# A mixer block on one Trainium2 core: five of seven column pairs of the MLP's first product as blocks of seven products

## The chip, the cores and the metric

One of the eight cores of a Trainium2 chip runs the whole kernel. The time is the device time of one execution in microseconds. Five engines work side by side, each on its own queue of instructions in program order: TensorE (PE; its weight loads are PEld) multiplies, VectorE (DVE), ScalarE (ACT) and GpSimd (POOL) work on elements, and SyncE (SP) issues most of the transfers. GpSimd issues those that add to what lies at their destination. SBUF holds the operands in 128 partitions; TensorE writes to PSUM, in banks of 512 float32 columns.

## What is computed

```python
x = A_x                                              # (1, 2048, 512)
h = x + attention(layernorm(x), wqkv, w_phi, wo)     # linear attention, 32 heads of 16
n = layernorm(h)
u = gelu(einsum("bsd,sf->bdf", n, w1) + b1)          # w1 (2048, 1792): over the tokens
y = einsum("bdf,fs->bds", u, w2) + b2                # w2 (1792, 2048)
out = h + transpose(y)
```

The MLP mixes tokens: its first product contracts 2048 tokens into 1792 features for each of 512 channels, its second contracts the features back into tokens. All is float32. A product is made of three passes of TensorE: each operand is split into a rounded high part (ScalarE's copy) and the rest (a subtraction, on VectorE or GpSimd), and high x high, high x low and low x high are summed in PSUM.

## The kernel before

The tokens stand in 16 tiles of 128, the features in 14 column tiles of 128. The work goes in four stages.

*Projections.* Keys, values and queries, with the layer norm folded into the weights. These are the same in both kernels.

*Attention, passes `it` = 0 to 17* (the loop over `it`). A pass works on several token tiles at once: `s_tr` and `s_num` make the numerators of a tile, `s_ol` its low part, `s_wo` the output projection into a bank `po` (L66 to L68, `mm3`), `s_h` adds the residual into `h` (L634) and stores it, and one pass later `s_moments`, `s_rstd` and `s_hn` normalize the tile and split it into `hs` (L61 and L62), one 128 x 512 operand for each of the high and the low part. The numerators and the projection share one bank, so the next `pn` waits for `s_h`. In the same passes `fill` already runs the MLP's first product for the first two column pairs: six products of 512 columns a call. The order on PE, DVE, ACT and POOL is the written one here.

*First product.* For each of seven pairs of column tiles `fill` runs through all 16 token tiles, 3 x 2 products of 512 columns for each. The weights come in by `stream` on SP's queue, ScalarE rounds them (L663), VectorE takes the rest (L670). `gelu` (L797) reads the finished banks; `operands_u` makes of the four quarters of a pair's result seven operands of 256 columns, by four subtractions (on GpSimd for the first two pairs, L804 to L807, and on VectorE for the others), and splits them.

*Second product.* Pairs of 128 x 128 blocks in both directions are multiplied by Strassen's and Winograd's scheme, with seven products of 256 columns in place of eight. `STEPS` are 8 pairs of token tiles x 7 pairs of feature tiles. `w2_sums` loads the raw blocks of two steps and makes three further sums in four operations (L854 to L857), `w2_parts` splits them, seven blocks of two steps at a time (L875, 1792 columns). `pair_of_tiles` multiplies: two of the products go by `narrow` (L913, three passes of 256 columns), five by `wide` (L921 with the high and the low part side by side, 512 columns, and L924, 256). The last pair of token tiles is all `narrow`. After a pair's seventh step VectorE and ScalarE sum the six banks (L972 to L988), and GpSimd issues adding stores of the result to `out` (L991, L992). `last_h` loads the last two tiles of `h` before the loop. Behind the attention the order is made by a planner, with `in_order` pinning the later part.

Of the kernel before, what the change touches and what calls it, by code (L numbers as in the profile page):

```python
# [17 lines left out]
P = 128  # L18
# [13 lines left out]
LAG = 3  # L32
WARM = 10
# [4 lines left out]
def block_kernel(ctx: ExitStack, tc: tile.TileContext, x, xT, wT, phic, wo, w1, b1, w2, b2,  # L38
# [34 lines left out]
    wqp = aq.enter_context(tc.tile_pool(name="wqp", bufs=1, side="right"))  # L73
    wqh = wqp.tile([P, KD, D], F32R, name="wqh")
    wql = wqp.tile([P, KD, D], F32R, name="wql")
    kvB = wqp.tile([P, 2, P], F32, name="kvB")
    kvS = wqp.tile([P, 4, 64], F32, name="kvS")
    sums = wqp.tile([P, SUMS, NPR, 2, 2], F32, name="smq")
    wqp.tile([P, 504], F32, name="pad")
# [378 lines left out]
    ms.enter_context(tc.manual_schedule(engines={ET.PE, ET.DVE, ET.Activation, ET.Pool}))  # L458
# [112 lines left out]
    ps_f = ctx.enter_context(tc.tile_pool(name="ps_f", bufs=2, space=PSUM, reuse_waits="tile"))  # L571
    wst = ExitStack()
# [5 lines left out]
    HN, HT, PHT, OS, PO, VE = {}, {}, {}, {}, {}, {}  # L578
# [68 lines left out]
    def s_hn(t):  # L647
        hn = ak.tile([P, D], F32, name="hn")
# [23 lines left out]
    def stream(src, k0, n, c0, w):  # L672

        raw = wf.tile([P, n, w], F32, name="wraw")
        wh_ = wf.tile([P, n, w], F32R, name="whi")
        wl_ = wf.tile([P, n, w], F32R, name="wlo")
# [44 lines left out]

    for it in range(NT + 2):
# [21 lines left out]
        if 0 <= it - 2 < NT:  # L744
            s_rstd(it - 2)
        if it + 3 < NT:
            s_ez(it + 3)
# [9 lines left out]
        run(sm if ql else sm[1:])  # L757
        if it > 0 and it + 2 < NT:
            run(s_den(it + 2, ps_t, "tr"))
        if 0 <= it - 1 < NT:  # L760
            s_wo(it - 1)
        for w in work[1:]:
            w()
        if 0 <= it - 1 < NT:
            s_h(it - 1)
        flush(1)
    flush()
    ms.close()
    a2.close()
    aq.close()  # L770

    NP = NF // 2
    HD = D // 2
    up = ctx.enter_context(tc.tile_pool(name="up", bufs=1, side="right", reuse_waits="tile"))
    uo = ctx.enter_context(tc.tile_pool(name="uo", bufs=2, side="right", reuse_waits="tile"))
    ws = ctx.enter_context(tc.tile_pool(name="ws", bufs=2, side="right", reuse_waits="tile"))
    ur = ctx.enter_context(tc.tile_pool(name="ur", bufs=4, side="right", reuse_waits="tile"))
    ut = ctx.enter_context(tc.tile_pool(name="ut", bufs=1, side="right", reuse_waits="tile"))
    ps_b = ctx.enter_context(tc.tile_pool(name="ps_b", bufs=4, space=PSUM, reuse_waits="tile"))
    NEAR = 2
    near = [up.tile([P, 7, 2, HD], F32R, name=f"un{p}") for p in range(NEAR)]  # L790
    up.tile([P, 120], F32, name="pad")
    U, UB, far = {}, {}, {}
# [7 lines left out]
    def operands_u(p):  # L800
        u = U[p]
        tt = ut.tile([P, 3, HD], F32, name="tt")
        e = nc.gpsimd if p < NEAR else nc.vector
        e.tensor_sub(tt[:, 0], u[:, 0], u[:, 1])  # L804
        e.tensor_sub(u[:, 0], u[:, 2], u[:, 0])
        e.tensor_sub(tt[:, 1], u[:, 2], tt[:, 0])
        e.tensor_sub(tt[:, 2], u[:, 3], tt[:, 1])  # L807
        if p < NEAR:
            for n0, src in ((0, u), (4, tt)):
                o = near[p][:, n0:n0 + src.shape[1]]  # L810
                split(o[:, :, 0], o[:, :, 1], src, nc.vector)
            for m in range(7):
                UB[p, m] = near[p][:, m]
            return
        for m in range(7):
            at = (p - NEAR) * 7 + m
            if at % 2 == 0:
                far[at // 2] = big.tile([P, 2, 2, HD], F32R, name="uf", tag="big")
            UB[p, m] = far[at // 2][:, at % 2]
            split(UB[p, m][:, 0], UB[p, m][:, 1], u[:, m] if m < 4 else tt[:, m - 4], nc.vector)  # L820

    for p in range(NP):
        while FN[p] < NT:
            fill(p, ps_b)
        for c in range(2):
            gelu(2 * p + c, PU[p][c])
        if p < NEAR:
            operands_u(p)
    for p in range(NEAR, NP):
        operands_u(p)  # L830
    wst.close()
    hp = ctx.enter_context(tc.tile_pool(name="hp", bufs=1, reuse_waits="tile"))

    STEPS = [(sp, p) for sp in range(NT // 2) for p in range(NP)]
    GRP = 2
    AW, RAW = {}, {}
    QUEUE = {}

    def in_order(*ops):

        for op in ops:
            with ExitStack() as st:
                for ins in QUEUE.values():
                    st.enter_context(tc.issue_after(ins))
                ins = op().ins
            QUEUE[ins.engine] = ins

    def w2_sums(g):
        other = g > AHEAD + 2 and g % 4 == 1
        raw = RAW[g] = (hp if other else ws).tile([P, GRP, 7, P], F32, name="wraw", bufs=1 if other else 3)  # L850
        for i, (sp, p) in enumerate(STEPS[g * GRP:(g + 1) * GRP]):
            nc.sync.dma_start(raw[:, i, 0:4].rearrange("p (k i) s -> p k (i s)", k=2),
                              w2v[:, 2 * p:2 * p + 2, sp * 2 * P:(sp + 1) * 2 * P])
        sums = (lambda: nc.vector.tensor_add(raw[:, :, 4], raw[:, :, 0], raw[:, :, 2]),  # L854
                lambda: nc.vector.tensor_sub(raw[:, :, 5], raw[:, :, 4], raw[:, :, 1]),
                lambda: nc.vector.tensor_sub(raw[:, :, 0], raw[:, :, 1], raw[:, :, 0]),
                lambda: nc.vector.tensor_sub(raw[:, :, 6], raw[:, :, 3], raw[:, :, 5]))  # L857
        if g < AHEAD:
            with tc.issue_after(LO[-18]):
                for op in sums:  # L860
                    op()
        else:
            in_order(*sums)

    def w2_parts(g):
        home = hp if g % 3 == 2 else ws
        wh_ = home.tile([P, GRP, 7, P], F32R, name="whi")
        wl_ = home.tile([P, GRP, 7, P], F32R, name="wlo")
        for i, step in enumerate(STEPS[g * GRP:(g + 1) * GRP]):
            AW[step] = wh_[:, i], wl_[:, i]  # L870
        raw = RAW.pop(g)
        if g < AHEAD:
            split(wh_, wl_, raw, nc.vector)
        else:
            in_order(lambda: nc.scalar.activation(wh_, raw, AF.Copy), lambda: nc.vector.tensor_sub(wl_, raw, wh_))  # L875

    AHEAD = 2
    for g in range(AHEAD):
        w2_sums(g)
        w2_parts(g)  # L880
    for g in range(AHEAD, AHEAD + 2):
        w2_sums(g)
    parts_next, sums_next = [], []

    def stream_w2(n):

        if (n + 1) % NP == 0:
            for g in sums_next:
                w2_sums(g)
            sums_next.clear()  # L890
        if n % GRP == 0:
            parts_next.append(n // GRP + AHEAD)
        if (n + 2) % NP == 0:
            return
        for g in parts_next:
            if g * GRP < len(STEPS):
                w2_parts(g)
            if (g + 2) * GRP < len(STEPS):
                if (n + 3) % NP == 0:
                    sums_next.append(g + 2)  # L900
                else:
                    w2_sums(g + 2)
        parts_next.clear()


    P1, P2, P3, P4, P5, P6, P7 = (1, 1), (3, 3), (6, 2), (2, 6), (4, 4), (5, 5), (0, 0)

    def narrow(o, ps, m, sp, opens, closes):

        for p in ps:  # L910
            wh_, wl_ = AW[sp, p]
            for i, (x, y) in enumerate(((wh_, 0), (wh_, 1), (wl_, 0))):
                in_order(lambda: nc.tensor.matmul(o, x[:, m[0]], UB[p, m[1]][:, y], start=opens and p == 0 and i == 0,  # L913
                                                  stop=closes and p == NP - 1 and i == 2, skip_group_check=True))

    def wide(sp, p, *products):


        wh_, wl_ = AW[sp, p]
        for o, m in products:  # L920
            in_order(lambda: nc.tensor.matmul(o, wh_[:, m[0]], UB[p, m[1]], start=p == 0, stop=False,  # L921
# [11 lines left out]
    def pair_of_tiles(sp, p):  # L933
# [6 lines left out]
        if t + 2 == NT:  # L940
            if p < NP - 3 or end:
# [5 lines left out]
                if end:  # L947
                    last_sums(t, HB)
# [126 lines left out]
```

## Time and profile before

| | |
|---|---|
| time, median of 2 runs | 519.69 us (519.3 to 520.09) |
| span of the profiled execution | 517.9 us |
| its time beside the span | the median is 1.8 us above the span; the profile has no time of its own beside this |
| TensorE busy | 513.2 us |
| VectorE busy | 395.0 us |
| ScalarE busy | 285.3 us |
| GpSimd busy | 235.9 us |
| granted TensorE clock | 1.00 throughout |
| transfers | 57.66 MB |

The span is from the first instruction to the last. A busy time counts overlapping matmuls once; a matmul of 512 columns has a duration of 0.39 us because it is pipelined, and the next one starts well before it ends. So the price of a matmul is the distance between two starts. The second product begins at about 376 us, the attention ends at about 262 us.

### The profile page before, as it was taken

How to read it: one execution, taken by the hardware profiler on the slowest of the kernel's cores; microseconds unless marked ns; L12 is line 12 of the kernel's file. 1: busy time of each engine (PE TensorE's matmuls, PEld its weight loads, DVE VectorE, ACT ScalarE, POOL GpSimd, SP SyncE). 2: the span in 40 equal slices, each digit the busy share in tenths (PEclk: the TensorE clock that was granted, in tenths of full speed). 3: DMA queues.
4: the chain of work that ended last, by engine and by line, in shares of the span. 5: the costliest groups of instructions: out<-in, count | busy, mean ns of one | idle time of the engine just before them, and what ended most of it. 6: DMA issues, size and time to landing. Idle time of an engine off the chain costs nothing.

```text
span 517.9 us, 9772 instructions
## 1 busy us (share of the span) xinstructions
PE 513.2 (99%) x3761; PEld 434.0 (84%) x3761; DVE 395.0 (76%) x719; ACT 285.3 (55%) x501; POOL 235.9 (46%) x182
## 2 busy tenths in 40 slices
PE   9999999999999999999999999999999999999997
PEld 8888888888887777777788888888899999999997
DVE  6799889989987899697336624625797899888993
ACT  6999853526267877767756423425464434433530
POOL 3579997876999999974224000000001102110210
PEclk9999999999999999999999999999999999999999
DMA  8642301021302334333255433532134586557732
GB/s 311 209 142 84 102 22 42 1 83 44 122 27 97 103 103 119 107 103 123 82 163 162 123 94 90 184 102 62 41 115 94 141 201 136 139 156 181 137 48 61
DMA packets 46493, 57.66 MB, mean 111 GB/s; under 512 B 4080, under 2 KB 33136, under 8 KB 46448
## 3 DMA queue, kind: packets, MB, share of 16 engines
q1 hardware_dynamic: 43136, 51.38, 31.4%
q0 software_dynamic: 3024, 5.51, 7.6%
q8 instruction: 29, 0.48, 0.4%
q10 hardware_dynamic: 288, 0.17, 0.1%
q14 instruction: 16, 0.13, 0.1%
HBM read 46.81 MB, written 10.22 MB: 110 GB/s over the span
## 4 chain that ended last, share of the span: by engine, by line
PE 97%; DVE 1%; ACT 1%; issue 0%; DVEq 0%
PE pu L66 13%; PE pu L68 12%; PE pu L67 12%; PE py L921 11%; PE py L913 10%; PE py L924 6%; PE po L66 3%; PE pk_ps L66 3%; PE po L68 3%; PE po L67 3%; PE pk_ps L67 3%; PE pk_ps L68 3%; PE pv L67 3%; PE pv L66 3%; PE pv L68 3%; PE tr L591 2%
## 5 line engine op out<-in xcount | busy, mean ns | idle before, releaser
L991 POOL DMA_DIRECT2D out<-ot x14 | 12.5, 941 | 170.3 <-DVE ot L972 170.3
L66 PE MATMUL pu<-hs,whi 128*128 128x512 f32 x224 | 87.7, 394 | 0.0
L67 PE MATMUL pu<-hs,whi 128*128 128x512 f32 x224 | 87.2, 389 | 0.0
L68 PE MATMUL pu<-hs,wlo 128*128 128x512 f32 x224 | 86.5, 389 | 0.0
L670 DVE TENSOR_TENSOR wlo<-wraw,whi 128x512 fp32r<-128x512 f32 x56 | 46.9, 841 | 46.5 <-ACT whi L663 46.2
L875 ACT ACTIVATE whi<-wraw 128x1792 fp32r<-128x1792 f32 x26 | 44.0, 1704 | 30.9 <-issue 17.4
L663 ACT ACTIVATE whi<-wraw 128x512 fp32r<-128x512 f32 x56 | 34.6, 625 | 44.4 <-PE pu L67 39.4
L875 DVE TENSOR_TENSOR wlo<-wraw,whi 128x1792 fp32r<-128x1792 f32 x26 | 52.4, 2019 | 0.0
L66 PEld LDWEIGHTS pu<-hs,whi 128*128 128x128 f32 x224 | 42.0, 188 | 9.1 <-ACT hj L641 0.2
L68 PEld LDWEIGHTS pu<-hs,wlo 128*128 128x128 f32 x224 | 42.0, 188 | 8.9
L67 PEld LDWEIGHTS pu<-hs,whi 128*128 128x128 f32 x224 | 42.1, 188 | 8.5
L921 PE MATMUL py<-uf,whi 128*128 128x512 f32 x175 | 48.4, 395 | 0.0
L484 POOL TENSOR_TENSOR ez<-eq,zB 128x1024 f32<-128x1024 f32 x16 | 38.4, 2405 | 3.8 <-ACT zB L544 3.8
L913 PE MATMUL py<-uf,whi 128*128 128x256 f32 x210 | 39.0, 283 | 0.0
L213 POOL TENSOR_TENSOR pk<-pk,sk 128x1024 f32<-128x1024 f32 x16 | 31.1, 1949 | 11.2 <-DVE sk L212 10.0
L508 POOL TENSOR_TENSOR eq<-eq,w 128x1024 f32<-128x1024 f32 x16 | 32.4, 2026 | 3.2 <-DVE w L505 3.2
L921 PEld LDWEIGHTS py<-uf,whi 128*128 128x128 f32 x175 | 30.1, 189 | 3.9
L913 PEld LDWEIGHTS py<-uf,whi 128*128 128x128 f32 x210 | 32.8, 192 | 0.0
L217 POOL TENSOR_TENSOR zacc<-zacc,pk 128x1024 f32<-128x1024 f32 x13 | 31.4, 2412 | 0.5
L924 PEld LDWEIGHTS py<-uf,wlo 128*128 128x128 f32 x175 | 27.1, 189 | 3.8
L913 PE MATMUL py<-uf,wlo 128*128 128x256 f32 x105 | 29.7, 283 | 0.0
L924 PE MATMUL py<-uf,wlo 128*128 128x256 f32 x175 | 28.7, 281 | 0.0
(200 smaller groups left out, 1303.9 us busy)
## 6 DMA issues: line engine op xcount, KB each, us to landing
wraw<-in_w SPq DMA_DIRECT2D x112, 256.0 KB, 3.0
xraw<-in_xT SPq DMA_DIRECT2D x16, 256.0 KB, 2.9
xh<-in_x SPq DMA_DIRECT2D x16, 256.0 KB, 2.6
h<-in_x SPq DMA_DIRECT2D x16, 256.0 KB, 2.7
out<-h SPq DMA_DIRECT2D x16, 256.0 KB, 2.1
out<-ot POOLq DMA_DIRECT2D x14, 256.0 KB, 4.4
wraw<-in_wT SPq DMA_DIRECT2D x12, 256.0 KB, 5.1
out<-low POOLq DMA_DIRECT2D x7, 256.0 KB, 4.2
```

The lines of the kernel that those rows point to most:

```text
L66: nc.tensor.matmul(o, ah, bh, start=first, stop=False)
L67: nc.tensor.matmul(o, ah, bl, start=False, stop=False)
L68: return nc.tensor.matmul(o, al, bh, start=False, stop=last).ins
L217: nc.gpsimd.tensor_add(zacc, zacc, PK[t])
L484: nc.gpsimd.tensor_mul(EZ[t], EQ[t], zB)
L508: nc.gpsimd.tensor_mul(heads(EQ[t]), heads(EQ[t]), W[t].rearrange("p g c h -> p (g c h)").unsqueeze(2).to_broadcast([P, 2 * H, DH]))
L663: nc.scalar.activation(wh_, raw, AF.Copy)
L670: LO.append(nc.vector.tensor_sub(wl_, raw, wh_).ins)
L875: in_order(lambda: nc.scalar.activation(wh_, raw, AF.Copy), lambda: nc.vector.tensor_sub(wl_, raw, wh_))
L913: in_order(lambda: nc.tensor.matmul(o, x[:, m[0]], UB[p, m[1]][:, y], start=opens and p == 0 and i == 0, stop=closes and p == NP - 1 and i ...
L921: in_order(lambda: nc.tensor.matmul(o, wh_[:, m[0]], UB[p, m[1]], start=p == 0, stop=False, skip_group_check=True))
L924: in_order(lambda: nc.tensor.matmul(o[:, 0], wl_[:, m[0]], UB[p, m[1]][:, 0], start=False, stop=p == NP - 1, skip_group_check=True))
```

## The change

The scheme of seven products now also takes five of the seven column pairs of the first product. Only the first two pairs (`PLAIN = 2`) still go by `fill`, up to token tile 14 in the attention's passes and with tile 15 after step 0. The other five run as 40 new steps in front of the 56 of the second product: 8 pairs of token tiles for each, 21 products of 256 columns per step (`products`), into four banks, of which there are two sets (`four_banks`). The first two row pairs of the second product go by `products` as well, interleaved; row pairs 2 to 6 go by `wide_step` as before, and the last by `last_step`.

For this the normalized tokens are kept unsplit too (`HF`), and their seven operands are made: `h_ops` (four subtractions of 256 columns for each pair of tiles, six on VectorE as a list `DQ` and two on GpSimd, four of the seven operands being the tile's own quarters, one of them replaced), and `h_parts`, which splits 768 columns of sums on ScalarE and VectorE and 256 columns on ScalarE and GpSimd (VectorE for pair 3).

The weight sums are fewer. `load_raw` loads a step's four blocks and one of them a second time (four transfers on SP's queue for two steps), `add_raw` adds two blocks to two of these on arrival (adding loads from GpSimd, two for two steps), and `w_sums` makes the remaining two sums on VectorE. `w_parts` splits one step at a time, two steps ahead, into three homes.

The gelu's operands come by `u_sums` (four subtractions on GpSimd for every pair) at fixed steps and `u_parts`. Everything behind the attention is in one written order on all five queues; a table `PENDING` says after which step what stands. The table of the gelu is loaded in pass 10.

```diff
+UR = 6
+PLAIN = 2
-        split(HN[t][:, 0], HN[t][:, 1], hn, nc.gpsimd)
+        split(HN[t][:, 0], HN[t][:, 1], hn, nc.gpsimd if t < NT - 1 else nc.vector)
...
+    def block_ops(e, v, t0, t1, t2):
+        return [lambda: e.tensor_sub(t0, v[0], v[1]), lambda: e.tensor_sub(v[0], v[2], v[0]),
+                lambda: e.tensor_sub(t1, v[2], t0), lambda: e.tensor_sub(t2, v[3], t1)]
+    STEPS = ([("u", p, j) for p in range(PLAIN, NP) for j in range(NT // 2)]
+             + [("y", sp, p) for sp, ps in ((0, (0, 1)), (1, (0, 1, 2, 3)), (0, (2, 3)), (1, (4, 5, 6)), (0, (4, 5, 6)))
+                for p in ps]
+             + [("y", sp, p) for sp in range(2, NT // 2) for p in range(NP)])
...
+        for k in range(2):
+            src, r, c = blocks(2 * g + k)
+            nc.sync.dma_start(RAW[g][:, k, 1:5].rearrange("p (k i) s -> p k (i s)", k=2),
+                              src[:, r:r + 2, c:c + 2 * P])
+            nc.sync.dma_start(RAW[g][:, k, 0], src[:, r + 1, c:c + P])
...
+            nc.gpsimd.dma_start(RAW[g][:, k, 0:2].rearrange("p i s -> p (i s)"), src[:, r, c:c + 2 * P],
+                                accum_op=ALU.add)
...
+        nc.vector.tensor_add(raw[:, :, 5], raw[:, :, 0], raw[:, :, 2])
+        nc.vector.tensor_add(raw[:, :, 6], raw[:, :, 4], raw[:, :, 5])
...
+        pool = (ws, ws2)[n % 3] if n % 3 < 2 else hp
+        PARTS[n] = pool.tile([P, 2, 7, P], F32R, name="wp")
+        split(PARTS[n][:, 0], PARTS[n][:, 1], RAW[n // 2][:, n % 2], nc.vector)
+    U_SUMS = {0: 25, 1: 29, 2: 35, 3: 37, 4: 39, 5: 41, 6: 44}
+    U_PARTS = {0: 33, 1: 35, 2: 37, 3: 39, 4: 41, 5: 43, 6: 46}
+    def h_parts(j):
+        v = HF.pop(j).rearrange("p i (k d) -> p (i k) d", k=2)
+        split(CB[j][:, :, 0], CB[j][:, :, 1], v[:, 1:4], nc.vector)
+        split(HN[2 * j][:, 0, 0:HD], HN[2 * j][:, 1, 0:HD], v[:, 0], nc.vector if j == 3 else nc.gpsimd)
...
     for it in range(NT + 2):
...
+        some(GQ, {14: 2, 15: 5, 16: 2}.get(it, 0))
...
+        if it in (11, 12):
+            load_raw(it - 11)
+        if it == 10:
+            nc.scalar.activation(mhalf[:, 1:2], mhalf[:, 2:3], AF.Gelu_apprx_tanh)
...
+        if it == 13:
+            for j in range(5):
+                DQ.extend(h_ops(j, nc.vector))
+            GQ.extend([lambda: add_raw(0)] + h_ops(5, nc.gpsimd) + [lambda: add_raw(1)])
+        if it == 15:
+            DQ.extend(h_ops(6, nc.vector))
+        if it == NT:
...
+            w_sums(0)
+            h_parts(0)
+            w_parts(0)
...
+    def products(n, banks, x, first, last):
+        a, b, c, d = banks
+        for o, m, opens in ((a[:, 0], P1, True), (a[:, 1], P6, False), (d[:, 0], P7, True), (b[:, 0], P5, True),
+                            (b[:, 1], P4, False), (c[:, 0], P3, True), (c[:, 1], P2, False)):
+            narrow(o, n, m, x(m[1]), first and opens, last)
...
+    at(len(STEPS) - 14, lambda: HB.extend(last_h(NT - 2)))
+    w_sums(1)
+    w_parts(1)
+    step(0)
+    for p in range(PLAIN):
+        fill(p)
+    load_raw(2)
+    load_raw(3)
+    h_parts(1)
+    add_raw(2)
+    some(h_ops(7, nc.gpsimd))
+    step(1)
+    for n in range(0, len(STEPS)):
+        if n > 1:
+            step(n)
+        w_parts(n + 2)
+        if n % 2 == 0:
+            load_raw(n // 2 + 4)
+            add_raw(n // 2 + 3)
+        else:
+            w_sums((n + 3) // 2)
+        if ready:
+            store()
+        for f in PENDING.pop(n, []):
+            f()
```

More of the change, by code (lines that the diff above doesn't have):

```diff
@@ L822, in block_kernel @@
[L822 to L861, printed above, removed]
-        else:
-            in_order(*sums)
@@ L865, in w2_parts @@
[L865 to L903, printed above, removed]
@@ L906, in block_kernel, with u_sums @@
[L906 to L919, printed above, removed]
+    def u_sums(p):
+        u, tt = U[p], hp.tile([P, 3, HD], F32, name="tt", bufs=2)
+        UT[p] = tt
+        some(block_ops(nc.gpsimd, [u[:, k] for k in range(4)], tt[:, 0], tt[:, 1], tt[:, 2]))
@@ new lines, in u_parts @@
+    def u_parts(p, i):
+        if i == 2:
+            o = cb_tile(p)
+            src = UT[p]
+        else:
+            o = big.tile([P, 2, 2, HD], F32R, name="uf", tag="big")
+            src = U[p][:, 2 * i:2 * i + 2]
+        for m in range(o.shape[1]):
+            UB[p, 2 * i + m] = o[:, m]
+        split(o[:, :, 0], o[:, :, 1], src, nc.vector)
+    for p in range(PLAIN):
+        while FN[p] < NT - 1:
+            fill(p)
+    a2.close()
+    cbb = ctx.enter_context(tc.tile_pool(name="cbb", bufs=1, side="right", reuse_waits="tile"))
@@ new lines, in block_kernel, with narrow @@
+    ps_b = ctx.enter_context(tc.tile_pool(name="ps_b", bufs=4, space=PSUM, reuse_waits="tile"))
+    for j in range(NT // 2):
+        if j not in CB:
+            CB[j] = cb_tile(j)
+    P1, P2, P3, P4, P5, P6, P7 = (2, 1), (4, 3), (6, 2), (3, 6), (0, 4), (5, 5), (1, 0)
+    def narrow(o, n, m, x, opens, closes):
+        wh_, wl_ = PARTS[n][:, 0], PARTS[n][:, 1]
+        for i, (w, y) in enumerate(((wh_, 0), (wh_, 1), (wl_, 0))):
+            nc.tensor.matmul(o, w[:, m[0]], x[:, y], start=opens and i == 0, stop=closes and i == 2, skip_group_check=True)
@@ new lines, in u_gelu, with y_out @@
+    def u_gelu(p):
+        for i in range(2):
+            v = flat(U[p][:, 2 * i:2 * i + 2])
+            nc.scalar.activation(v, v, AF.Gelu_apprx_tanh, bias=b1s[:, 2 * p + i:2 * p + i + 1])
+    def y_out(t, banks):
+        e, u3 = firsts(banks)
+        ot = ur.tile([P, 4, HD], F32, name="u")
+        for i, a in enumerate((u3, e)):
+            nc.vector.scalar_tensor_tensor(ot[:, 2 * i:2 * i + 2], banks[1 + i], b2s[:, t + i:t + i + 1], a,
+                                           op0=ALU.add, op1=ALU.add)
+        return [(t + i, ot[:, 2 * i:2 * i + 2]) for i in range(2)]
@@ L990, in pair_of_tiles @@
-        for i in range(2):
-            nc.gpsimd.dma_start(out[(t + i) * P:(t + i + 1) * P, :], flat(ot[:, i]), accum_op=ALU.add)
-        nc.gpsimd.dma_start(out[(t + 1) * P:(t + 2) * P, :], flat(low), accum_op=ALU.add)
+        if NP - 3 <= p < NP - 1:
+            return []
+        places = [(b16[:, 0], P1, True), (b16[:, 1], P6, False), (b7[:, 0], P7, True), (b5[:, 0], P5, True),
+                  (b4[:, 0], P4, True), (b3[:, 0], P3, True), (b2[:, 0], P2, True)]
+        for o, m, opens in places if end else places[5:] + places[:5]:
+            for k in range(2 if end else 0, -1, -1):
+                narrow(o, n - k, m, UB[p - k, m[1]], opens and p == 0, end and k == 0)
@@ new lines, in block_kernel, with later, at @@
+    PENDING = {}
+    def later(d, f):
+        PENDING.setdefault(now[0] + d, []).append(f)
+    now = [-3]
+    def at(n, f, *args):
+        PENDING.setdefault(n, []).append(lambda: f(*args))
+    for j in range(2, NT // 2):
+        at(j - 2, h_parts, j)
+    for p in range(PLAIN):
+        for c in range(2):
+            at(c + 3, gelu, 2 * p + c, PU[p][c])
+    for p, n in U_SUMS.items():
+        at(n, u_sums, p)
+    for p, n in U_PARTS.items():
+        at(n, u_parts, p, 0)
+        at(n, u_parts, p, 1)
+        at(n + 1, u_parts, p, 2)
@@ new lines, in block_kernel @@
+    at(len(STEPS) - 14, lambda: HB.extend(last_h(NT - 2)))
+    HB = []
+    w_sums(1)
+    w_parts(1)
+    step(0)
+    for p in range(PLAIN):
+        fill(p)
+    wst.close()
+    hp = ctx.enter_context(tc.tile_pool(name="hp", bufs=1, reuse_waits="tile"))
+    load_raw(2)
[5 more added lines that the diff above has]
+    for n in range(0, len(STEPS)):
+        now[0] = n
+        ready = len(STORES)
+        if n > 1:
[4 more added lines that the diff above has]
+            add_raw(n // 2 + 3)
+        else:
+            w_sums((n + 3) // 2)
[3 more added lines that the diff above has]
+            f()
```

288 lines of the change are left out of this document (171 added, 117 removed).

## The prediction

> **What bounds the kernel now.** I read the page first, then the chain of waits, then TensorE's timeline, then the other engines where the change lands.
>
> ```profile
> span 517.9 us, 9772 instructions
> PE 513.2 (99%) x3761; PEld 434.0 (84%) x3761; DVE 395.0 (76%) x719; ACT 285.3 (55%) x501; POOL 235.9 (46%) x182
> PE 97%; DVE 1%; ACT 1%; issue 0%; DVEq 0%
> ```
>
> TensorE is the bound from start to end, and there are almost no holes to fill: any gain must come from fewer or cheaper matmuls, and any wait of TensorE for operands is added to the time in full. So I price the matmuls first, by their spacing and not by their pipelined duration. The timeline gives eighteen products of 512 columns in a row, the chain the steps of the second product.
>
> ```profile
> 250.73 0.40 PE L66 MATMUL po<-woh,oh 128*128 128x512 f32 x1
> ...
> 254.60 0.39 PE L68 MATMUL pu<-hs,wlo 128*128 128x512 f32 x1
> ...
> 259.72 0.39 PE L68 MATMUL po<-woh,ol 128*128 128x512 f32 x1
> 378.17 1.15 PE py L921 x5
> 380.63 1.16 PE py L921 x5
> 496.79 17.65 PE py L913 x147
> ```
>
> 3.87 us over 17 gaps is 0.228 us for 512 columns; 17.65 / 147 is 0.120 us for 256 columns. A step of the second product is 2.46 us, an all-narrow step of 21 products 21 x 0.120 = 2.52 us.
>
> **Parts 1 and 2: the matmuls.** The first product loses ten of its fourteen column tiles: 10 x 16 x 3 = 480 products of 512 columns, 480 x 0.228 = 109.4 us. It gains five pairs x 8 steps x 21 = 840 narrow ones, 100.8 us. The first two row pairs of the second product turn narrow, 14 steps x 0.06 = 0.8 us more. TensorE's own work falls by 109.4 - 100.8 - 0.8 = 7.8 us. That is all that the arithmetic saves, because each narrow product carries 0.12 us for half the columns of 0.228.
>
> **What the operands cost.** The new steps want splits and sums that the plain fill did not. The groups by line and shape give their durations.
>
> ```profile
> L875 DVE TENSOR_TENSOR wlo<-wraw,whi 128x1792 fp32r<-128x1792 f32 x26 | 52.4, 2019 | 0.0
> L855 DVE TENSOR_TENSOR wraw<-wraw 128x256 f32<-128x256 f32 x28 | 11.9, 424 | 0.8
> L875 ACT ACTIVATE whi<-wraw 128x1792 fp32r<-128x1792 f32 x26 | 44.0, 1704 | 30.9 <-issue 17.4 <-PE py L913 8.7 <-DVE wraw L857 4.8
> L663 ACT ACTIVATE whi<-wraw 128x512 fp32r<-128x512 f32 x56 | 34.6, 625 | 44.4 <-PE pu L67 39.4 <-DVE wraw L856 2.1 <-issue 1.8
> L991 POOL DMA_DIRECT2D out<-ot x14 | 12.5, 941 | 170.3 <-DVE ot L972 170.3
> ```
>
> On VectorE 256 elements take 0.42 us and 1792 take 2.02, so 1.04 ns an element: 896 (`w_parts`, one per step) 1.09 us, 768 (`h_parts`, the third part of `u_parts`) 0.95, 512 0.69. On ScalarE 896 takes 0.95, 768 0.84. `w_sums` is two adds of 256, 0.85 us every second step. A GpSimd issue of an adding load holds GpSimd 0.9 us, and there is one per step.
>
> VectorE and GpSimd do not run freely beside each other. The two timelines show it:
>
> ```profile
> 254.34 0.69 DVE L670 TENSOR_TENSOR wlo<-wraw,whi 128x512 fp32r<-128x512 f32 x1
> 231.69 1.95 POOL L508 TENSOR_TENSOR eq<-eq,w 128x1024 f32<-128x1024 f32 x1 [0.43 <-DVE w L505]
> 232.17 2.01 DVE L670 TENSOR_TENSOR wlo<-wraw,whi 128x512 fp32r<-128x512 f32 x1
> 274.83 0.74 POOL L807 TENSOR_TENSOR tt<-u,tt 128x256 f32<-128x256 f32 x1
> 280.11 0.69 DVE L670 TENSOR_TENSOR wlo<-wraw,whi 128x512 fp32r<-128x512 f32 x1
> 280.27 1.12 POOL L804 TENSOR_TENSOR tt<-u 128x256 f32<-128x256 f32 x1 [4.70 <-DVE un L62]
> ```
>
> The same subtraction takes 0.69 us alone and 2.01 us when GpSimd's multiplication began before it: it ends just 0.54 us after that one. GpSimd's subtraction of 256 takes 0.74 alone and 1.12 behind VectorE's. Each waits out the other, so I add their times. [...]
>
> **Part 3: the end of the attention.** `h_ops` puts 28 subtractions (28 x 0.42 = 11.8 us) on VectorE and four (3.0 us) with four adding loads (3.6 us) on GpSimd into the last four passes, and the activation table of the gelu moves to pass 10.
>
> ```profile
> 242.57 0.68 DVE L618 TENSOR_TENSOR ol<-pn,oh 128x512 fp32r<-128x512 f32 x1
> 246.74 0.69 DVE L634 SCALAR_TENSOR_TENSOR h<-po,h 128x512 f32<-128x512 f32 x1 [3.50 <-PE po L68]
> 264.86 0.63 ACT L61 ACTIVATE hs<-hn 128x512 fp32r<-128x512 f32 x1
> 270.09 1.28 ACT L797 ACT_TABLE_LOAD   x1
> ```
>
> VectorE idles 3.5 us between `ol` and `h` of a pass, so the work fits by volume. But TensorE waits for `h` (it frees the bank for `pn`) and for `ol`, and a subtraction in front of either costs up to 0.42 us, or 1.3 with GpSimd's split under way: eight such waits at about half a microsecond, 4 us, and the table load 1 of its 1.28. SP's queue takes eight loads of raw weights in passes 11 and 12, between a store of `h` and a load of `x` that is wanted passes later; I put nothing for it. I take 5; bounds 0 (all slip into the idle time) and 9.
>
> **Part 4: the first eight block steps.** From 259.72 + 0.23 eighteen more fill products run to 264.0, where step 0 stands. Steps 0 to 7 and the last two fills (12 x 0.228) want 8 x 2.52 + 2.7 = 22.9 us of TensorE. The last token tile's normalized rows come at 265.5 (the ScalarE row at 264.86); three copies of block 0 now stand ahead of it on ScalarE (0.84 + 0.41 + 0.95), so it comes near 267.3. Behind it, in VectorE's written order: its own split 0.7, four `w_sums` 3.4, seven `w_parts` 7.6, seven `h_parts` 6.7 and one of 0.42; on GpSimd six splits of a block's first 256 columns (the quarter split) 4.4 and `h_ops(7)` 3.0. Together 26.2 us, so step 7's operands stand at 293.5, while TensorE would want them at 264.0 + 17.7 + 2.7 = 284.4. The loss is 9.1 us. The first to be seen should be step 2, whose quarter split stands on GpSimd behind two adding loads, `h_ops(7)` and two more adding loads, 3.6 + 3.0 us. Taken 9, bounds 4 (times do not add) and 12.
>
> **Part 5: the gelu's operands, steps 33 to 47.** Fifteen steps are 37.8 us of TensorE. VectorE has fifteen `w_parts` 16.4, eight `w_sums` 6.8, seven `u_parts` of 0.69 + 0.69 + 0.95 = 16.3 and `u_out` 2.7; GpSimd has five `u_sums` of four subtractions, 20 x 0.74 = 14.8. The sum is 57.0, 19.2 over. Weights are split two steps ahead, which hides 5.0 us: 14 us are lost. If GpSimd's part were free, 42.2 us against 37.8 would vanish in the 5.0: bounds 0 and 19.
>
> **Part 6: the wide steps.** VectorE's sums at the end of a pair are one burst:
>
> ```profile
> 426.31 0.42 DVE L981 TENSOR_TENSOR u<-py,e 128x256 f32<-128x256 f32 x1 [0.99 <-ACT e L979]
> ...
> 429.61 0.87 DVE L972 SCALAR_TENSOR_TENSOR ot<-py,b2s,e 128x256 f32<-128x256 f32 x2
> 411.02:497.00 85.98, 85.98 (x560) 78.41 (x560) 78.37 (x136) 36.48 (x38) 13.07 (x15) 1.00 0.63 144
> ```
>
> The burst is 4.2 us. Now the parts of step n+2 stand behind it (before, two groups were ready): 1.3 us until the first bank is done + 4.2 + 1.09 = 6.6 us after the step's start, wanted after 2 x 2.46 + 1.16 (five wide products first) = 6.1. That is 0.5 to 1 us for each of five pairs, 4. The first wide pair waits for banks that `y_out` frees, a copy and three sums late: 2. The last pair opens narrow and has no 1.16 in front: 2. `last_h`, now at step 82, makes VectorE wait in line for two loads of 256 KB (2.8 us by the next fence) that stand on SP's queue behind four others, in the middle of a burst: 4, bounds 1 and 6. Together 12, bounds 5 and 16.
>
> **Part 7: the transfers.** Rows of the issues, and of the queues between 411.02 and 497:
>
> ```profile
> q0 software_dynamic: 2160, 3.93, 32.4%
> q1 hardware_dynamic: 8704, 8.39, 30.4%
> u<-out SPq DMA_DIRECT2D x2, 256.0 KB, 2.8
> ```
>
> Plain loads cost 0.304 x 86 / 8.39 = 3.1 us of all sixteen engines per MB, adding stores 0.324 x 86 / 3.93 = 7.1. A wide pair of 17.3 us now loads 2.29 MB (7.1 us), stores 0.79 MB (5.6) and adds 0.92 MB, which no row prices: 2.9 us as plain loads, 6.5 as adding stores. That is 15.6 to 19.2 us of 17.3. The adds are nearer to the adding stores, but four raw groups in flight absorb the first excess: 3, bounds 0 and 13 (five pairs of 1.9, and the queue's lateness).
>
> **The sum.** 517.9 - 7.8 + 5 + 9 + 14 + 12 + 3 = 553.1 us of span. The median of the runs shown, 519.69, is 1.8 above the span, for what lies around it: 555 us.
>
> **The rivals.** *GpSimd's subtractions find gaps of their own.* VectorE waits about 0.95 us for ScalarE's copy before each split; if GpSimd fits there, part 5 falls to 1, part 4 to 5 and part 3 to 3, and the rest stays: 519.7 - 7.8 + 3 + 5 + 1 + 12 + 3 = 536 us. Against it: in parts 4 and 5 the queues are full. *The adding loads bound the wide steps*, 13 in place of 3: 565 us. For it the 7.1 us per MB, against it that VectorE's lateness already thins the demand. *TensorE stays the bound*: two steps of lead, the banks in two sets and the late gelu cover it all, so that of 43 us of waits under 10 remain; it is decided at step 2 and in steps 33 to 47, where everything must arrive within 2.52 us a step. Then 519.7 - 7.8 = 512 us, up to 522 with what remains. For it: GpSimd is idle in most of this stage and TensorE waited for nothing before. *The narrow products do not keep 0.120 us* with the new operands: at 0.135 the saving becomes 5 us of loss, and 568 with the waits; the 147 of the row above, same shapes, speak against it.
>
> **How the numbers follow.** The forecast, 540 to 563, gets 0.55; gaps on GpSimd 0.16; adding loads 0.10; TensorE bound 0.16; slower products 0.03. Two per cent, about what a measurement of this kernel can tell, is 509.3 to 530.1. The third rival reaches both sides: 0.05 faster, 0.11 within, and 0.03 of the second group also ends within. So 0.05, 0.14, 0.81. The range holds 8 of 10: low 524, high 570.
>
> **What would show it.** Right: TensorE's busy share falls to about 92%, with waits at step 2 for GpSimd's quarter split, a row of waits for VectorE's weight split in steps 38 to 47, and one for it near step 85; GpSimd's 256-element subtractions above 0.74 us. Wrong: a chain that is again 97% TensorE, weight splits ready two steps ahead through steps 33 to 47, or DMA engines over 95% busy with VectorE waiting for `RAW`.

## The result and the profile after

| | before | after |
|---|---|---|
| time, median of the runs shown | 519.69 us | 557.38 us (557.29 to 557.47) |
| ratio, 95% interval | | 1.0725, 1.0704 to 1.0745 |
| span of the profiled execution | 517.9 us | 555.4 us |

The changed kernel is 7% slower. The page, its lines for the span, the busy times and the granted clock:

```profile
span 555.4 us, 11271 instructions
PE 523.0 (94%) x4191; PEld 458.4 (83%) x4191; DVE 453.8 (82%) x742; ACT 307.4 (55%) x527; POOL 354.3 (64%) x310
PEclk9999999999999999998989999999799999999799
```

TensorE's busy share fell from 99 to 94%. The last line is new: before, the granted clock was full throughout; now four slices show an 8 or a 7. A matmul at half clock still counts as busy (from 258.90 to 265.73 us TensorE is busy for 6.00 of the 6.83 us at a clock of 0.50), so the busy time overstates the work. The waits, TensorE's (waiting line, releaser, total us, times, longest us):

```profile
PE py L920 <- DVE wp L66: 7.3, 6, 2.6
PE py L929 <- DVE wp L66: 6.2, 5, 4.9
PE py L920 <- POOL hs L66: 5.0, 1, 5.0
PE pn L615 <- DVE h L640: 4.4, 3, 2.8
```

These are the four places that the prediction names. Of the first row 5.3 us lie in steps 40, 42 and 46, where VectorE's weight split stands among the gelu's operands; of the second 4.9 us lie in step 85, behind `last_h`; the third is GpSimd's quarter split at step 2, and the fourth the residual add in the attention. Before, TensorE had no wait like the first three, and this of the fourth kind:

```profile
PE pn L609 <- DVE h L634: 0.2, 1, 0.2
```

Where the time lies is read from the stretches. The first line below is the attention's last product into `po` in TensorE's timeline, which started at 259.72 before. Each line under it is a stretch: its bounds and its length, the busy us of PE, PEld, DVE, ACT and POOL, the clock, and the DMA share and GB/s. The bounds are starts of steps: 0, 8, 33, 48, the first wide pair, and the last pair.

```profile
267.08 0.39 PE L72 MATMUL po<-woh,ol 128*128 128x512 f32 x1
271.40:304.20 32.80, 26.84 (x181) 25.12 (x180) 26.13 (x28) 20.26 (x34) 20.65 (x21) 0.90 0.64 144
304.20:367.20 63.00, 63.00 (x527) 63.00 (x526) 46.01 (x69) 28.10 (x34) 30.15 (x34) 1.00 0.82 184
367.20:415.30 48.10, 41.48 (x318) 40.71 (x317) 46.61 (x55) 27.39 (x40) 32.76 (x34) 0.93 0.63 144
415.30:430.40 15.10, 15.10 (x127) 15.10 (x127) 12.33 (x20) 6.72 (x9) 7.06 (x8) 1.00 0.72 160
430.40:531.20 100.80, 92.03 (x563) 80.69 (x562) 71.21 (x122) 37.80 (x54) 43.84 (x50) 0.97 0.99 209
531.20:555.40 24.20, 18.70 (x149) 17.79 (x147) 14.84 (x28) 6.42 (x9) 2.98 (x4) 1.00 0.38 64
```

Steps 8 to 32 and 48 to 53 run with no gap: 25 steps in 63.0 us, 2.52 us each. The rest is longer than TensorE's own work:

| stretch | own work or before, us | after | excess | of it half clock |
|---|---|---|---|---|
| to the last `po` | 259.7 | 267.1 | 7.4 | 3.0 |
| steps 0 to 7, with the last fills | 22.9 | 32.8 | 9.9 | 2.8 |
| steps 33 to 47 | 37.8 | 48.1 | 10.3 | 3.0 |
| five wide pairs | 86.0 | 100.8 | 14.8 | 2.6 |
| last pair and the end | 20.9 | 24.2 | 3.3 | 0 |

The excess is 45.7 us; less the 7.8 us of work saved that is 37.9, and the spans differ by 37.5. The last column counts the time that TensorE worked at half clock, halved (products of 512 columns start 0.43 us apart there, in place of 0.228): the record of the clock shows 0.5 for 6.83 us from 258.9, 286.2, 395.4 and 518.3 us on, and the waits under way there ended at 259.7, 287.4, 396.3 and 520.1. This column is a reckoning, and not what a full clock would have gained: in steps 33 to 47 VectorE is busy for 46.6 of the 48.1 us, so a faster TensorE would have waited longer there.

### The profile page after: what moved, and what is told of

It reads as the page before. It is cut to its first block, busy times and chain, and to the rows that moved or that the text cites. A ratio compares the mean times of both kernels' runs of the same rounds, so it can differ in the third digit from the quotient of the medians.

```text
span 555.4 us, 11271 instructions
## 1 busy us (share of the span) xinstructions
PE 523.0 (94%) x4191; PEld 458.4 (83%) x4191; DVE 453.8 (82%) x742; ACT 307.4 (55%) x527; POOL 354.3 (64%) x310
## 5 line engine op out<-in xcount | busy, mean ns | idle before, releaser
L65 ACT ACTIVATE wp<-wraw 128x896 fp32r<-128x896 f32 x96 | 89.5, 949 | 136.1 <-PE py L920 50.8
L775 POOL DMA_DIRECT2D wraw<-in_w x96 | 87.9, 1050 | 91.3 <-DMA wraw<-in_w 50.4
L66 DVE TENSOR_TENSOR wp<-wraw,wp 128x896 fp32r<-128x896 f32 x96 | 106.5, 1126 | 44.7 <-ACT wp L65 44.7
L920 PE MATMUL py<-cb,wp 128*128 128x256 f32 x654 | 106.5, 289 | 0.6 <-DVE cb L66 0.6
L920 PEld LDWEIGHTS py<-cb,wp 128*128 128x128 f32 x654 | 92.4, 198 | 1.0 <-DVE cb L66 1.0
L920 PE MATMUL py<-hs,wp 128*128 128x256 f32 x480 | 72.9, 287 | 5.0 <-POOL hs L66 5.0
L920 PEld LDWEIGHTS py<-hs,wp 128*128 128x128 f32 x480 | 65.2, 196 | 5.6 <-POOL hs L66 5.2
L920 PE MATMUL py<-uf,wp 128*128 128x256 f32 x357 | 59.1, 292 | 8.9 <-DVE wp L66 7.3
L920 PEld LDWEIGHTS py<-uf,wp 128*128 128x128 f32 x357 | 50.6, 199 | 10.5 <-DVE wp L66 8.6
L218 POOL TENSOR_TENSOR pk<-pk,sk 128x1024 f32<-128x1024 f32 x16 | 31.0, 1943 | 11.2 <-DVE sk L217 10.1
L927 PE MATMUL py<-uf,wp 128*128 128x512 f32 x105 | 33.0, 406 | 2.0 <-DVE u L970 1.1
L929 PEld LDWEIGHTS py<-uf,wp 128*128 128x128 f32 x105 | 18.1, 196 | 11.4 <-DVE wp L66 8.4
L929 PE MATMUL py<-uf,wp 128*128 128x256 f32 x105 | 20.8, 293 | 6.2 <-DVE wp L66 6.2
L194 ACT ACTIVATE pk<-pk,r 128x1024 f32<-128x1024 f32 x16 | 18.4, 1148 | 14.9 <-DVE pk L172 14.4
L70 PE MATMUL po<-woh,oh 128*128 128x512 f32 x64 | 25.8, 403 | 0.1
```

The source lines that it names most:

```text
L65: nc.scalar.activation(hi, src, AF.Copy)
L66: lo_engine.tensor_sub(lo, src, hi)
L70: nc.tensor.matmul(o, ah, bh, start=first, stop=False)
L218: nc.gpsimd.tensor_mul(heads(PK[t]), heads(PK[t]), sk.unsqueeze(2).to_broadcast([P, 2 * H, DH]))
L775: nc.gpsimd.dma_start(RAW[g][:, k, 0:2].rearrange("p i s -> p (i s)"), src[:, r, c:c + 2 * P], accum_op=ALU.add)
L920: nc.tensor.matmul(o, w[:, m[0]], x[:, y], start=opens and i == 0, stop=closes and i == 2, skip_group_check=True)
```

## The experiments

All times below stand against 557.4 us of the changed kernel and 519.7 of the one before, which ran beside each of them (519.72 and 519.73). The changed kernel has two runs, 0.2 us apart. The four runs of one experiment's kernel spread by up to 6 us (third experiment: 549.2 to 555.6, mean clock 0.978 to 0.988), so I read the stretches of the profile first and the medians second.

**One: `u_sums` on VectorE.**

```diff
-        some(block_ops(nc.gpsimd, [u[:, k] for k in range(4)], tt[:, 0], tt[:, 1], tt[:, 2]))
+        some(block_ops(nc.vector, [u[:, k] for k in range(4)], tt[:, 0], tt[:, 1], tt[:, 2]))
```

> Edit: the four subtractions of u_sums go to VectorE in place of GpSimd; nothing else. Theory (VectorE and GpSimd exclude each other, so their times add in steps 33 to 47): each of 20 subtractions there costs 0.42 us on VectorE in place of 0.74 on GpSimd, 6.4 us less for the two engines together. The waits for weight splits and gelu operands between 384 and 410 us in the changed kernel are 7.3 us, and the half clock from 395.4 us costs another 3.4; expected 557.4 - 5 to 9 = 548 to 552 us. Rival (GpSimd's subtractions find gaps of their own beside VectorE): VectorE only gets 20 x 0.42 = 8.4 us more to do, and the time goes up to 558 to 566 us.

Measured: 556.6 us (554.9 to 557.3), ratio 1.0715 (1.0697 to 1.0733). Neither expectation holds in the median. Steps 33 to 47, the same steps as the two rows of the first fence below taken together, take 44.6 us in place of 48.1; the half clock there lasted 3.4 us in place of 6.8 (a clock of 0.94 over 26.9 us in place of 0.89 over 30.4), so of the 3.5 us 2.2 are waits. The first fence is of this kernel, the second groups the form of the subtraction (line 733) in the changed kernel between 364 and 416 us, with shortest, median and longest duration in ns.

```profile
365.40:383.10 17.70, 17.70 (x150) 17.70 (x149) 17.46 (x30) 13.40 (x19) 5.40 (x7) 1.00 0.77 167
383.10:410.00 26.90, 22.63 (x170) 21.84 (x169) 25.31 (x44) 13.46 (x21) 6.95 (x8) 0.94 0.56 127
```

```profile
L733 POOL TENSOR_TENSOR tt<-u x5: 1122/1512/1517, 373.9 to 404.7; 128x256 f32<-128x256 f32 x5
L733 POOL TENSOR_TENSOR u<-u x5: 793/801/806, 375.5 to 405.9; 128x256 f32<-128x256 f32 x5
```

VectorE took on 20 x 0.42 = 8.4 us and the waits still became 2.2 us shorter, so GpSimd's 20 subtractions had cost it about 10.6 us, 0.53 each and not the 0.74 that I added. VectorE's own rows agree. These are its splits of 512 elements in the stage (busy us, mean ns), in the changed kernel and here:

```profile
L66 DVE TENSOR_TENSOR uf<-u,uf 128x512 fp32r<-128x512 f32 x13 | 13.8, 1099 | 0.0
L66 DVE TENSOR_TENSOR uf<-u,uf 128x512 fp32r<-128x512 f32 x12 | 7.7, 686 | 0.0
```

The two sums of `w_sums` likewise last 0.84 and 0.72 us in place of 0.42 and 0.43; over these 27 instructions that is 10.4 us. So the subtractions do hold VectorE up, and VectorE them (the first of each four lasts 1.5 us, behind a split of VectorE), but nearly three tenths of their time cost VectorE nothing. The median hardly moved because the steps behind gave 2.8 us back (0.6 in steps 48 to 53, 2.2 in the wide pairs), and because the half clocks vary (mean clock 0.978 to 0.982 in the four runs).

**Two: the quarter split on VectorE.**

```diff
-        split(HN[2 * j][:, 0, 0:HD], HN[2 * j][:, 1, 0:HD], v[:, 0], nc.vector if j == 3 else nc.gpsimd)
+        split(HN[2 * j][:, 0, 0:HD], HN[2 * j][:, 1, 0:HD], v[:, 0], nc.vector)
```

> Edit: the quarter split of h_parts goes to VectorE for every pair of tiles, in place of GpSimd for all but pair 3. Theory: the wait of 5.0 us at step 2 comes only from the place in GpSimd's queue, behind four adding loads and h_ops(7); it goes, and with it the half clock from 286.2 us (3.4 us). VectorE gets 6 x 0.42 = 2.5 us more, in the steps where it is full, so 2 to 3 us come back in later waits. Expected 557.4 - 5 - 3.4 + 2.5 = 551.5 us, 549 to 554. Rival (VectorE's own list of splits is the bound of steps 0 to 7, whoever makes the quarter): the wait moves to the next split, and the time is 556 to 560 us.

Measured: 553.3 us (551.6 to 554.5), ratio 1.0644 (1.0616 to 1.0672), within the theory's 549 to 554. The wait at step 2 is gone. What stood in front of it is seen in GpSimd's timeline of the changed kernel (start, duration, line, operation; in brackets the idle time before and its releaser):

```profile
276.28 1.16 POOL L66 TENSOR_TENSOR hs<-u,hs 128x256 fp32r<-128x256 f32 x1 [3.80 <-ACT hs L65]
277.39 1.78 POOL L775 DMA_DIRECT2D wraw<-in_w  x2
278.56 3.69 POOL L733 TENSOR_TENSOR hf<-hf 128x256 f32<-128x256 f32 x2
282.33 2.31 POOL L734 TENSOR_TENSOR hf<-hf 128x256 f32<-128x256 f32 x2
284.59 1.77 POOL L775 DMA_DIRECT2D wraw<-in_w  x2
285.74 1.57 POOL L66 TENSOR_TENSOR hs<-u,hs 128x256 fp32r<-128x256 f32 x1
```

Two adding loads, the four subtractions of `h_ops(7)` at 6.0 us in place of the 3.0 that they cost alone, two more adding loads, then the split that TensorE wants. Steps 0 to 7 fall from 32.8 to 27.8 us, and the run's mean clock rises from 0.975 to 0.985. In the 4.9 left over 22.9 every wait that the profile names ends with an operation of VectorE: that is its own list.

**Three: `last_h`'s additions later.**

```diff
-            nc.vector.tensor_scalar(hb[:, i], hb[:, i], b2s[:, t + i:t + i + 1], None, op0=ALU.add)
...
+    def last_b2(t):
+        for i in range(2):
+            nc.vector.tensor_scalar(HB[i], HB[i], b2s[:, t + i:t + i + 1], None, op0=ALU.add)
...
+    at(len(STEPS) - 5, last_b2, NT - 2)
```

> Edit: last_h still issues its two loads at step 82, but VectorE's two additions of b2 to them stand after step 91. Theory: VectorE stands in line for the loads (5.6 us) with the weight splits of the next steps behind it; that makes the wait of 4.9 us of TensorE near 515 us and the half clock from 518.3 us. Without it 4.9 + 3.4 = 8 us less, less what the burst at the pair's end still costs (1): expected 549 to 551 us. Rival (the transfers are full there, and the weights come late whoever waits): the wait goes over to the weights, and the time is 555 to 558 us.

Measured: 553.1 us (549.2 to 555.6), ratio 1.0636 (1.0589 to 1.0683). Less was gained than the theory says. VectorE's timeline of the changed kernel, then of this one, shows why:

```profile
517.87 1.12 DVE L1057 TENSOR_SCALAR u<-u,b2s 128x512 f32<-128x512 f32 x2 [5.57 <-DMA u<-out]
518.91 1.08 DVE L66 TENSOR_TENSOR wp<-wraw,wp 128x896 fp32r<-128x896 f32 x1
```

```profile
518.88 1.08 DVE L66 TENSOR_TENSOR wp<-wraw,wp 128x896 fp32r<-128x896 f32 x1
522.93 0.43 DVE L783 TENSOR_TENSOR wraw<-wraw 128x256 f32<-128x256 f32 x1 [2.97 <-DMA wraw<-in_w]
```

The 5.57 us behind the load of `h` are gone and the last wide pair falls from 25.8 to 18.4 us. But now the next thing is late: a group's adding loads, 2.97 us in front of the weight sums, with the pair's sums queued behind. The last pair with the end takes 28.9 us in place of 24.2, at a clock of 0.87 in place of 1.00, and TensorE is busy in it for 21.9 us in place of 18.7. Theory and rival each had a part of it.

**Four: pauses and the clock.** The core of a kernel with trains of products and pauses:

```diff
+            for i in range(count):
+                nc.tensor.matmul(o, a, b, start=i == 0, stop=i == count - 1)
...
+            for i in range(chain - 2):
+                nc.scalar.activation(junk[:, :widths[r]], junk[:, :widths[r]], AF.Copy)
...
+            nc.vector.scalar_tensor_tensor(b, junk, 1e-6, raw, op0=ALU.mult, op1=ALU.add)
```

> A kernel of its own that leaves out all of the reference's computation: 36 trains of 85 to 115 products of 512 columns, and after each a chain of one to six operations on ScalarE and VectorE that TensorE waits for, so that it stands still for about 1 to 5 us. [...] Rival one: the length of the pause alone decides, at a fixed length between 1.9 and 2.8 us. [...]

Measured: 942.7 us, with a mean granted clock of 0.971. Three pauses from TensorE's timeline (the bracket is the idle time), then stretches around eight pauses, these three among them, with the clock:

```profile
206.77 6.45 PE L62 MATMUL o<-b,a 128*128 128x512 f32 x20 [1.81 <-DVE b L70]
281.00 5.28 PE L62 MATMUL o<-b,a 128*128 128x512 f32 x22 [2.99 <-DVE b L70]
588.27 3.02 PE L62 MATMUL o<-b,a 128*128 128x512 f32 x12 [3.42 <-DVE b L70]
```

```profile
112.00:119.00 7.00, 4.72 (x14) 3.45 (x13) 0.69 (x1) 1.37 (x4) 0.00 (x0) 0.76 0.00 0
136.00:144.00 8.00, 5.43 (x25) 4.17 (x24) 0.69 (x1) 1.62 (x5) 0.00 (x0) 1.00 0.00 0
204.00:212.00 8.00, 6.19 (x21) 4.64 (x20) 0.69 (x1) 0.96 (x2) 0.00 (x0) 0.79 0.00 0
253.00:261.00 8.00, 5.40 (x24) 4.15 (x23) 0.69 (x1) 1.68 (x4) 0.00 (x0) 1.00 0.00 0
277.00:286.00 9.00, 6.01 (x27) 4.66 (x26) 0.69 (x1) 2.05 (x5) 0.00 (x0) 1.00 0.01 2
555.00:563.00 8.00, 5.08 (x16) 3.79 (x15) 0.69 (x1) 2.00 (x4) 0.00 (x0) 0.79 0.00 0
584.00:593.00 9.00, 5.58 (x25) 4.30 (x24) 0.69 (x1) 2.47 (x5) 0.00 (x0) 1.00 0.00 0
748.00:758.00 10.00, 6.37 (x21) 4.78 (x20) 0.69 (x1) 2.69 (x5) 0.00 (x0) 0.83 0.00 1
```

The pause of a row is its length less PE's busy time. Beside pauses of 1.81, 2.28, 2.92 and 3.63 us the clock is 0.76 to 0.83, about 1.7 us lost in each row, or 3.4 us at 0.5; beside pauses of 2.57, 2.60, 2.99 and 3.42 us it is 1.00. So the rival with the length alone falls: no length parts the one group from the other. What else decides was not shown.

The changed kernel's four falls lasted 6.83 us each, and each began in a wait of TensorE: of 2.77, 5.04, 2.55 and 4.89 us. Its longest other wait from 20 us on, 1.64 us before 386.90, had no fall. Why a fall lasts 6.83 us there and about 3.4 us here was not shown either.

**Five: no `h_ops`.**

```diff
-        return block_ops(e, [v[:, k] for k in range(4)], v[:, 1], v[:, 2], v[:, 3])
+        return []
```

> Leaves out the 32 subtractions of h_ops (24 on VectorE, 8 on GpSimd with those of the last pair), so the block operands are the plain quarters; all else is as in the changed kernel. Theory: these subtractions, in front of the residual add and the low parts in VectorE's written order, are what makes the attention end at 267.1 in place of 259.7 us, and h_ops(7) is most of what the quarter split at step 2 waits for (3.0 of 5.0 us). The attention ends at 260 to 263 us, the long waits at 257 and 282 us go with their half clocks; expected 557.4 - 5 - 5 = 547 us, 545 to 550. Rival (the table load, the eight raw loads on SP's queue and the adding loads make the attention's end late): it still ends at 266 or later, and only step 2 is shorter, 552 to 554 us.

Measured: 548.5 us (547.8 to 551.7), ratio 1.0565 (1.0533 to 1.0596), as the theory had it. The last `po` of this kernel:

```profile
260.48 0.39 PE L72 MATMUL po<-woh,ol 128*128 128x512 f32 x1
```

It stands 0.8 us behind that of before, and the products ahead of it, from 258.64 us on, start 0.23 us apart; in the changed kernel, at half clock, those at 261.36 and 261.79 us start 0.43 apart. So the subtractions, with the half clock beside their wait, are nearly the whole late end of the attention; the table load and SP's queue are not. The wait for the quarter split at step 2 falls from 5.0 to 0.2 us.

**Six: the third experiment without adding loads.**

```diff
-            nc.gpsimd.dma_start(RAW[g][:, k, 0:2].rearrange("p i s -> p (i s)"), src[:, r, c:c + 2 * P],
-                                accum_op=ALU.add)
+            pass
```

> The third experiment (last_h's additions late) and no adding loads: the weight sums lack two blocks, the 96 adding loads are left out, the second load of a block stays. Theory of the prediction (the adds cost 3 us, 0 to 13, absorbed by four groups in flight): against the third experiment (553.1 us) -2 to -5 us, all of it in the wide steps and behind them, where its VectorE waits 3.0 us at 520 us for a group's blocks: 548 to 551 us, a wide pair at 17.5 to 18 us. Rival (the full transfers bound the wide steps): -8 to -13 us, 540 to 545 us, a wide pair at 17.2 as before. Rival two (nothing waits for the transfers): 552 to 554 us.

Measured: 541.5 us (541.2 to 541.7), ratio 1.0417 (1.0399 to 1.0434), 11.5 us less than the third experiment, but not where the rival that fits the number has it. Four wide pairs, of the third experiment and of this one:

```profile
449.50:522.30 72.80, 70.77 (x450) 62.77 (x449) 53.89 (x92) 30.61 (x44) 34.38 (x39) 1.00 1.01 219
```

```profile
442.90:515.40 72.50, 70.79 (x451) 62.79 (x450) 55.50 (x97) 30.60 (x44) 10.44 (x12) 1.00 0.73 172
```

With transfers at a share of 1.01 and at 0.73, the wide pairs take the same 18.2 us: full transfers are not their bound. The time went mainly at three other places: 4.7 us in the last pair (28.9 us at a clock of 0.87 to 24.2 at 1.00), 2.7 in steps 0 to 7 (the wait for the quarter split is 2.4 in place of 5.0 us), and 3.0 in the attention (a part of it half clock: from 262.52 to 263.38 us products of the third experiment start 0.43 us apart, and those of this one from 259.91 to 262.21 us 0.23), whose last `po` starts at 262.2 and not at 265.2. Steps 33 to 47 gave 1.6 more, and steps 8 to 32 lost 0.8. At the second and the third place it is GpSimd's queue. VectorE and GpSimd in the attention of the changed kernel, then of this one:

```profile
252.71 1.68 POOL L734 TENSOR_TENSOR u<-u 128x256 f32<-128x256 f32 x2
254.33 1.79 POOL L775 DMA_DIRECT2D wraw<-in_w  x2
255.51 1.92 POOL L66 TENSOR_TENSOR hs<-hf,hs 128x512 fp32r<-128x512 f32 x1
254.71 3.48 DVE L734 TENSOR_TENSOR u<-u 128x256 f32<-128x256 f32 x2
258.89 0.68 DVE L640 SCALAR_TENSOR_TENSOR h<-po,h 128x512 f32<-128x512 f32 x1
```

```profile
253.34 1.41 POOL L66 TENSOR_TENSOR hs<-hf,hs 128x512 fp32r<-128x512 f32 x1
253.63 1.86 DVE L734 TENSOR_TENSOR u<-u 128x256 f32<-128x256 f32 x2
256.20 0.69 DVE L640 SCALAR_TENSOR_TENSOR h<-po,h 128x512 f32<-128x512 f32 x1
```

Two of VectorE's subtractions, 0.87 us by themselves, last 3.48 beside two adding loads and GpSimd's split, and 1.86 beside the split alone; TensorE's `pn` waits for the `h` behind them.

**Seven: the first three, and `h_ops(7)` on VectorE behind step 3.** The edits of experiments one to three, and:

```diff
-    some(h_ops(7, nc.gpsimd))
+    at(3, lambda: some(h_ops(7, nc.vector)))
```

> The first three experiments together, and h_ops(7) on VectorE behind step 3: no GpSimd subtraction stands behind the attention. Theory: the gains add, about 1 + 4 + 4 us and 2 more for h_ops(7); half clocks that no longer come give some of it twice, transfers that bound the end take some back: 546 us, 543 to 549. VectorE stays the bound of steps 0 to 7 (24.6 us of work against 22.9) and 40 to 47. Rival (each fix moves the wait to the next one in line): 551 to 554 us.

Measured: 542.0 us (538.8 to 543.6), ratio 1.0420 (1.0383 to 1.0457), 15.3 us less than the changed kernel: 1.0 below the theory's range. The mean clock is 0.993 in place of 0.975, about 7.6 us at half clock in place of 27.3. Steps 0 to 7 take 26.8 us, steps 33 to 47 44.5. It is the fastest whole version of the changed kernel here, and 22 us slower than the kernel before.

**Eight: the seventh without low parts of the weights.** The second change stands in `narrow` and in `wide`.

```diff
-        split(PARTS[n][:, 0], PARTS[n][:, 1], RAW[n // 2][:, n % 2], nc.vector)
+        nc.scalar.activation(PARTS[n][:, 0], RAW[n // 2][:, n % 2], AF.Copy)
...
-        wh_, wl_ = PARTS[n][:, 0], PARTS[n][:, 1]
+        wh_, wl_ = PARTS[n][:, 0], PARTS[n][:, 0]
```

> The seventh experiment's kernel, and w_parts makes only the high part: the 96 subtractions of 896 on VectorE are left out, and the products take the high part in place of the low one, the same number of products of the same shape. Theory (VectorE's own volume is what is left of the loss): 1.09 us less for each step; steps 0 to 7 and 40 to 47 fall to TensorE's own 20 us, the wide steps to 17.2 to 18 us a pair, the attention's late end (7 us) and the transfers at the end (4 us) stay: 512 + 7 + 4 + 2 to 5 = 525 to 528 us. Rival (latencies of the written order and not the volume, or dearer products): above 535 us.

Measured: 523.0 us (521.5 to 524.3), ratio 1.0061 (1.0040 to 1.0083). The same stretches as of the changed kernel:

```profile
269.40:293.40 24.00, 23.47 (x182) 22.51 (x181) 15.86 (x32) 19.90 (x34) 9.23 (x11) 1.00 0.87 201
356.40:394.20 37.80, 37.80 (x317) 37.80 (x317) 29.82 (x60) 29.23 (x41) 13.41 (x17) 1.00 0.78 179
409.30:497.70 88.40, 87.60 (x563) 79.05 (x562) 30.32 (x76) 37.89 (x52) 42.41 (x49) 1.00 1.04 228
```

Without that share of VectorE's work, steps 33 to 47 take exactly TensorE's 37.8 us, steps 0 to 7 24.0 and the wide pairs 88.4. So the loss in these stages is the weight split on VectorE, and the products are not dearer. In steps 0 to 7 and 33 to 47 it is VectorE's volume: in the seventh experiment VectorE was busy for 17.8 of the last 18.0 us of the first stage, and for 42.7 of the 44.5 us of the second. In the wide pairs it was busy for only 65.7 of 88.6 us, so there the place of the split in the queue may count as much as its length; this experiment takes away both, and does not tell them apart. What stays is the attention (265.1 against 259.7), 1.1 us in steps 0 to 7, 2.4 in the wide pairs and 2.4 at the end: 11.3, less 7.8 is 3.5, and the spans differ by 3.1. Even with VectorE's largest item gone the change only breaks about even.

## Why the prediction was right, and where its steps were off

The time came within 2.4 us of the 555 forecast. TensorE's own work came as worked out (63.0 us for 25 steps), and the four places of waiting are the ones named, step 2's GpSimd split first. The sizes are another matter. That the total came so near is luck in part: the half clock, which was not in the sum, filled up terms that were too large.

| term | predicted, us | waits alone | with half clock |
|---|---|---|---|
| part 3, attention | 5 | 4.4 | 7.4 |
| part 4, steps 0 to 7 | 9 | 7.1 | 9.9 |
| part 5, steps 33 to 47 | 14 | 7.3 | 10.3 |
| parts 6 and 7, wide steps, transfers | 15 | 15.5 | 18.1 |
| sum | 43 | 34.3 | 45.7 |

*Part 3* has the right place, as the fifth experiment shows, and a miscount: `h_ops` of six pairs are 24 subtractions on VectorE, not 28 (10.1 us). The table load was no part of it; the adding loads on GpSimd, whose waits I put at nothing here, were, though only beside the subtractions: the fifth experiment keeps these loads and its attention ends 0.8 us late.

*Part 4*: the order of the queues was right. The adding loads and `h_ops(7)` were to delay step 2 by 3.6 + 3.0 us; the wait was 5.0. VectorE's own list stayed as 4.9 us when the GpSimd split was gone.

*Part 5* came to half of its 14 us if the waits alone are counted, to three quarters with the half clock. GpSimd's 14.8 us were added in full; the first experiment puts their cost at about 10.6. With that, 52.8 us of work against 37.8, less the lead of 5.0, is 10. The 42.2 of VectorE was too large as well, since durations do not add up there either: in the first experiment's stage its 73 instructions last 47.1 us together and VectorE is busy for 42.8, because one starts about 0.08 us before the one ahead has ended. How much of the rest the lead of two steps hides, no run here shows.

*Part 6*: `last_h` cost 4.9 us (4 predicted), the first wide pair's banks about 2 (2), the last pair's 3.3 (2).

*Part 7* was right in sum and wrong in mechanism. Full transfers cost next to nothing (72.8 us of four wide pairs with them, 72.5 without); the adding loads cost GpSimd's time (in four wide pairs it is busy for 34.4 us with them, 10.4 without), and a late group shows only once `last_h` is out of the way.

Two figures of the prediction are off without an effect on the forecast. VectorE and GpSimd do not wait each other out in full: in the rows shown each ends 0.15 us earlier than full waiting would have it. And products at 0.135 us would have made the saving a loss of 9 us and not of 5, since the first two row pairs of the second product turn narrow too.

Of the rivals, slower products and TensorE as the bound are refuted by the 63.0 us and by the waits, the adding loads as bound of the wide steps by the sixth experiment. GpSimd's gaps of their own are real, for nearly three tenths of its time in part 5.

## What to carry to other kernels

A change that saves a bound engine 7.8 us of 520 can take on very little work of the other engines: here it put 58.8 us on VectorE (395.0 to 453.8, with the time that GpSimd held it up), much of it in stages where each step leaves 2.5 us. Add up every engine's work by stage and not over the span, with VectorE's and GpSimd's SBUF subtractions largely in one sum (in part 5 GpSimd's 14.8 us cost about 10.6); look for short queues that hold something urgent behind something that could wait (step 2, `last_h`); and when one such wait is mended, look for what is late next before counting the gain.

## What the runs showed of the hardware

In the changed kernel the granted clock fell to 0.5 four times, for 6.83 us each, beginning in waits of TensorE of 2.55 to 5.04 us; by the reckoning above that was 11.4 us of TensorE's time beside the waits. The starts lie 27.3, 109.2 and 122.9 us apart, 4, 16 and 18 times 6.83 us. In the fourth experiment's kernel a pause of 1.81 us stands beside a fall and one of 3.42 us beside none. The mean clock does not order the times of one kernel: in the third experiment 0.978 stands beside 553.0 us and 0.981 beside 555.6.

The issue of an adding load did not by itself hold VectorE up: in the changed kernel from 225 us on, 107 of its subtractions and additions in SBUF run beside such issues and no subtraction of GpSimd, and each is within 0.02 us of the shortest of its shape. Why two VectorE subtractions lasted 3.48 us beside two adding loads and a split was not settled.
